# Linear attention with a smooth-ReLU MLP: an instruction order fixed by a list scheduler, transposes split between TensorE and DMA, and a new order of loads

## The chip, the cores and the metric

The kernel runs on one core of a Trainium2 chip. The metric is device time in microseconds (us), the median of several executions. The engines are named as the profile names them: PE (TensorE; PEld is its weight load), DVE (VectorE), ACT (ScalarE), POOL (GpSimd) and SP (SyncE, which here only issues DMA transfers; SPq is its queue).

## What is computed

The attention part is a linear recurrence over S = 768 steps for B = 4 batches, H = 8 heads and D = 48 channels; the MLP part takes the 3072 resulting rows of 384 numbers through 2048 hidden units and back.

```python
for t in range(S):                      # r, k, v: (4, 8, 768, 48); w, u: (8, 48)
    cur = np.einsum('bhd,bhe->bhde', u[None] * kt, vt)
    y[:, :, t] = np.einsum('bhd,bhde->bhe', rt, state + cur)
    state = w[None, :, :, None] * state + np.einsum('bhd,bhe->bhde', kt, vt)
x = y.transpose(0, 2, 1, 3).reshape(3072, 384)
h = x @ w_in                            # 384 -> 2048
g = np.where(h >= 1, h, np.where(h <= -1, 0.0, (h + 1) ** 2 / 4))
out = g @ w_out                         # 2048 -> 384, float32
```

## The kernel before

**Units.** The 768 steps are cut into 6 chunks of 128. A *unit* is one chunk of one batch, 128 rows by 8 heads; there are 24, chunk by chunk, the four batches inside a chunk. Two units make one MLP block of 256 rows, so there are 12 blocks. Unit i of batch b needs the state that unit i - 4 leaves.

**A unit's attention** is five calls:

- `prep` (L172 to L181): the unit's K, R and V (float32, 128 x 8 x 48, 192 KB each, loaded in pieces of 192 bytes) become K * Winv and R * Wpow (powers of w along the chunk, so that the decay becomes a product), in bfloat16 and padded from 48 to 64 columns a head; K * u * R, whose sum over a head is the diagonal term; and V in bfloat16. K * Winv and both products of K * u * R are on POOL; R * Wpow on DVE for units 0 to 5, later on POOL; V's cast on ACT for units 0 to 7, later on POOL.
- `s_tr` (L188, L190): eight 128 x 128 transposes on PE (two heads each) into PSUM, and a copy of all of them on ACT (L192) to a tile RK, which holds R and K transposed.
- `s_at` (L202): eight small matmuls, K against R, give the scores AT; DVE multiplies them with the causal mask (L206, two halves), and sums K * u * R over each head (L209). The next unit that is not yet loaded is loaded from here.
- `s_y`: y from the state (L220) and from AT and V (L223); the unit's own contribution to the state, st (L231); on DVE x = V * diagonal + y, head by head, eight instructions (L234); the state T is updated (L242, L244 on DVE, the decay L245 on POOL) and cast to Tbd (L248, ACT).
- `s_xp`: three transposes of x on PE (L255), a copy to xT (L257, ACT) and a sum of squares for a bound on |h| (L259, ACT).

**The MLP.** `layer1(m, n)` is one eighth of block m's hidden units: six matmuls (L270) and, on ACT, one Square (L276), which is the middle branch of the activation. `layer2(m, n)` is four matmuls (L288), two for each unit of the block; after the eighth piece the two outputs are copied (L292, one on DVE, one on ACT) and stored (L295). `w_norms` (L303 to L313) and `bound_fails` compute whether any |h| can pass 1; only then is the MLP done again with the full activation, which does not happen with this data.

**Weights.** w_in and w_out come as four quarters of 768 KB each (L106, L111) and are cast to bfloat16 by DVE and ACT (L337, L343).

**What sets the order.** The calls stand in the program in an order written by hand: one by one for blocks 0 to 2, then from a table `plan`, which puts the stages of unit i beside certain pieces of the MLP. All of it stands in one block, inside which the framework orders the instructions of each engine and the DMA issues by a model of its own of their times:

```python
    man.enter_context(tc.block(schedule_with_timeline_sim=True))
    ...
        g = max(m * nP - 15 + 4 * j, G0 - 5 + 3 * (i - 4 * UB))
        for s, at in enumerate((0, 2, 4, 7, 9)):
            plan.setdefault(max(g + at, G0), []).append((s, i))
```

Every DMA is issued from SP. K, R and V have six buffers each, the transposed and masked tiles three, the weights' float32 quarters four; of PSUM's eight banks the attention has four, layer 1 two and layer 2 two.

Of the kernel before, what the change touches and what calls it, by code (L numbers as in the profile page):

```python
# [11 lines left out]
ALU = mybir.AluOpType  # L12


@with_exitstack
def kernel(
# [11 lines left out]
    nc = tc.nc  # L28
# [13 lines left out]
    NB = B * NCH // UB  # L42
    LIM = 0.95
    mm = nc.tensor.matmul

    const = ctx.enter_context(tc.tile_pool(name="const", bufs=1))
    stage = ctx.enter_context(tc.tile_pool(name="stage", bufs=4))
    io = ctx.enter_context(tc.tile_pool(name="io", bufs=6))
    work = ctx.enter_context(tc.tile_pool(name="work", bufs=3))
    gpool = ctx.enter_context(tc.tile_pool(name="gpool", bufs=3))  # L50
    ewp = ctx.enter_context(tc.tile_pool(name="ewp", bufs=3))
    ps_h = ctx.enter_context(tc.tile_pool(name="ps_h", bufs=2, space=bass.MemoryType.PSUM))
    ps_o = ctx.enter_context(tc.tile_pool(name="ps_o", bufs=2, space=bass.MemoryType.PSUM))
    ps_a = ctx.enter_context(tc.tile_pool(name="ps_a", bufs=4, space=bass.MemoryType.PSUM))

    man = ExitStack()
    man.enter_context(tc.block(schedule_with_timeline_sim=True))


    units = [(b, c) for c in range(NCH) for b in range(B)]  # L60
    loaded = {}
    next_load = [0]

    def load():
        i = next_load[0]
        if i == len(units):
            return
        next_load[0] += 1
        b, c = units[i]
        t0 = c * C  # L70
        tiles = []
        for name, src in (("K", k), ("R", r), ("V", v)):
            t = io.tile([128, H, D], F32, name=name, tag=name)
            nc.sync.dma_start(out=t, in_=src[b, :, t0 : t0 + C, :].rearrange("h s d -> s h d"))
            tiles.append(t)
        loaded[i] = tiles
# [5 lines left out]
    nc.sync.dma_start(out=w_bc, in_=row_bcast(w))  # L82

    wc = const.tile([128, NP], F32, name="wc")
    nc.vector.memset(wc, 1.0)
    with nc.allow_non_contiguous_dma(reason="384 words"):
        for s in range(2):
            nc.sync.dma_start(
                out=wc[s * DP : s * DP + D, :],
                in_=w.rearrange("(p s) d -> s d p", s=2)[s],  # L90
            )
    load()
    u_bc = const.tile([128, H * D], F32, name="u_bc")
    nc.sync.dma_start(out=u_bc, in_=row_bcast(u))
    load()

# [6 lines left out]
    w_in_f, w_out_f = [], []  # L103
    for q in range(NQ):
        t = stage.tile([128, nKb, FQ], F32, name="w_in_f", tag="wf")
        nc.sync.dma_start(out=t, in_=w_in_src[:, :, q * FQ : (q + 1) * FQ])  # L106
        w_in_f.append(t)
        load()
    for q in range(NQ):
        t = stage.tile([128, TQ, d_out], F32, name="w_out_f", tag="wf")  # L110
        nc.sync.dma_start(out=t, in_=w_out_src[:, q * TQ : (q + 1) * TQ, :])  # L111
        w_out_f.append(t)


    ident = const.tile([128, 128], BF16, name="ident")
    make_identity(nc, ident)
    umask = const.tile([128, 128], F32, name="umask")
    nc.gpsimd.memset(umask, 0.0)
    nc.gpsimd.affine_select(
        out=umask, in_=umask, compare_op=ALU.is_ge, fill=1.0,  # L120
        base=0, pattern=[[-1, 128]], channel_multiplier=1,
    )
    ones = const.tile([128, 1], BF16, name="ones")
    nc.vector.memset(ones, 1.0)
    i_int = const.tile([128, 1], mybir.dt.int32, name="i_int")
    nc.gpsimd.iota(i_int, pattern=[[0, 1]], base=0, channel_multiplier=1)
    i_col = const.tile([128, 1], F32, name="i_col")
    nc.vector.tensor_copy(i_col, i_int)
    negj_col = const.tile([128, 1], F32, name="negj_col")
    nc.vector.tensor_scalar(negj_col, i_col, -1.0, -1.0, ALU.mult, ALU.add)  # L130
    lw = const.tile([128, H * D], F32, name="lw")
    nc.scalar.activation(lw, w_bc, AF.Ln)
    nc.scalar.activation(wc, wc, AF.Ln)
    Wpow = const.tile([128, H, D], F32, name="Wpow")
    nc.scalar.activation(Wpow.rearrange("p h d -> p (h d)"), lw, AF.Exp, scale=i_col)
    Winv = const.tile([128, H, D], F32, name="Winv")
    nc.scalar.activation(Winv.rearrange("p h d -> p (h d)"), lw, AF.Exp, scale=negj_col)  # L137
    nc.scalar.activation(wc, wc, AF.Exp, scale=float(C))
# [6 lines left out]
    NR = 4  # L145
    RWp, KWi = [], []
    for i in range(NR):
        for lst, nm in ((RWp, "RWp"), (KWi, "KWi")):
            t = const.tile([128, H, DP], BF16, name=f"{nm}{i}")
            nc.vector.memset(t, 0.0)  # L150
            lst.append(t)

    T = [const.tile([128, NP, D], F32, name=f"T{b}") for b in range(B)]
    Tbd = []
    for b in range(B):
        nc.gpsimd.memset(T[b], 0.0)
        t = const.tile([128, NP, 2 * D], BF16, name=f"Tbd{b}")
        nc.gpsimd.memset(t, 0.0)
        Tbd.append(t)
    xT = [const.tile([128, nKb, MT], BF16, name=f"xT{m}") for m in range(NB)]  # L160
    xn = const.tile([128, len(units)], F32, name="xn")
# [5 lines left out]
    ut = {}  # L167

    def prep(i):
        K, R, Vf = loaded.pop(i)  # L170
        Rw, Kw = RWp[i % NR], KWi[i % NR]
        nc.gpsimd.tensor_mul(Kw[:, :, 0:D], K, Winv)  # L172
        (nc.vector if i < 6 else nc.gpsimd).tensor_mul(Rw[:, :, 0:D], R, Wpow)
        KU = work.tile([128, H, D], F32, name="KU", tag="KU")
        nc.gpsimd.tensor_mul(KU, K, u3)  # L175
        nc.gpsimd.tensor_mul(KU, KU, R)  # L176
        V = work.tile([128, H, D], BF16, name="V", tag="V")
        if i < 8:
            nc.scalar.copy(V, Vf)
        else:  # L180
            nc.gpsimd.tensor_copy(V, Vf)  # L181
        ut[i] = [Rw, Kw, V, KU]

    def s_tr(i):
        Rw, Kw, V, KU = ut[i]
        tr = ps_a.tile([128, 2 * NP, 128], BF16, name="tr", tag="a")
        for p in range(NP):
            nc.tensor.transpose(tr[:, NP + p, :], pair(Kw, p), ident)  # L188
        for p in range(NP):
            nc.tensor.transpose(tr[:, p, :], pair(Rw, p), ident)  # L190
        RK = work.tile([128, 2 * NP, 128], BF16, name="RK", tag="RK")
        nc.scalar.copy(RK, tr)  # L192
        ut[i] = [Kw, V, RK, KU]

    def s_at(i):
        Kw, V, RK, KU = ut[i]
        RT, KT = RK[:, 0:NP, :], RK[:, NP : 2 * NP, :]
        AT_p = [ps_a.tile([128, NP, 128], F32, name=f"AT_p{s}", tag="a") for s in range(2)]
        for p in range(NP):
            for s in range(2):  # L200
                rows = slice(s * DP, s * DP + D)
# [143 lines left out]
    def each(m, ns, layer):  # L345
        for n in ns:
            layer(m, n)
# [142 lines left out]
```

## Time and profile before

| | |
|---|---|
| median of 3 runs | 200.91 us (200.70, 200.91, 202.21) |
| span of the profiled execution | 197.9 us (3.0 less than the median; its own time is this span and what lies around it, which the page does not show) |
| PE busy | 173.8 us, 88% of the span, 1818 matmuls |
| ACT, DVE, POOL busy | 136.0, 113.0 and 110.3 us |
| moved by DMA | 25.94 MB; most packets are under 512 bytes |

The page gives busy times, then the span in 40 slices, then the chain of work that ended last, then the costliest groups of instructions by line. The times are of one execution; the groups and the windows are means over many instructions. A line number is that of the kernel above.

### The profile page before, as it was taken

How to read it: one execution, taken by the hardware profiler on the slowest of the kernel's cores; microseconds unless marked ns; L12 is line 12 of the kernel's file. 1: busy time of each engine (PE TensorE's matmuls, PEld its weight loads, DVE VectorE, ACT ScalarE, POOL GpSimd, SP SyncE). 2: the span in 40 equal slices, each digit the busy share in tenths (PEclk: the TensorE clock that was granted, in tenths of full speed). 3: DMA queues.
4: the chain of work that ended last, by engine and by line, in shares of the span. 5: the costliest groups of instructions: out<-in, count | busy, mean ns of one | idle time of the engine just before them, and what ended most of it. 6: DMA issues, size and time to landing. Idle time of an engine off the chain costs nothing.

```text
span 197.9 us, 4831 instructions
## 1 busy us (share of the span) xinstructions
PE 173.8 (88%) x1818; PEld 129.5 (65%) x1818; DVE 113.0 (57%) x358; ACT 136.0 (69%) x275; POOL 110.3 (56%) x144
## 2 busy tenths in 40 slices
PE   0263697789999999999999999999999999999990
PEld 0141584677877677866687787686787777777750
DVE  4179999993777707952637647538457654331110
ACT  3657779899797826964787977866677776454540
POOL 7498664979797999994667846927513100000000
PEclk9999999999999999999999999999999999999999
DMA  4999999979999999999984400111011011020202
GB/s 97 200 253 262 252 232 182 257 134 246 223 213 267 176 187 174 254 187 237 228 182 81 120 3 23 59 39 45 2 43 40 3 40 43 0 80 0 84 3 89
DMA packets 82782, 25.94 MB, mean 131 GB/s; under 512 B 75841, under 2 KB 81217, under 8 KB 82753
## 3 DMA queue, kind: packets, MB, share of 16 engines
q1 hardware_dynamic: 82752, 25.57, 58.4%
q8 instruction: 16, 0.26, 0.6%
q14 instruction: 14, 0.11, 0.2%
HBM read 20.84 MB, written 4.72 MB: 129 GB/s over the span
## 4 chain that ended last, share of the span: by engine, by line
PE 67%; ACT 5%; DMA 3%; DVE 3%; issue 1%; ACTq 0%
PE o_p L288 30%; PE h_p L270 24%; DMA w_out_f<-in_moe_w_out_dram 3%; PE y L223 2%; ACT gT L276 2%; PE tr L190 2%; PE tr L188 2%; PE xp L255 1%; DVE x L234 1%; PE y L220 1%; PE st L231 1%; ACT RK L192 1%; PE n_p L309 1%; ACT w_out_sb L343 0%; DVE T_189 L242 0%
## 5 line engine op out<-in xcount | busy, mean ns | idle before, releaser
L276 ACT ACTIVATE gT<-h_p 128x512 bf16<-128x512 f32 x96 | 57.0, 598 | 38.1 <-PE h_p L270 37.3
L288 PE MATMUL o_p<-w_out_sb,gT 128*128 128x384 bf16 x384 | 73.5, 326 | 0.0
L270 PEld LDWEIGHTS <-w_in_sb 128*128 128x128 bf16 x576 | 53.8, 99 | 12.6 <-issue 1.0
L234 DVE SCALAR_TENSOR_TENSOR x<-V,diag,y 128x48 bf16<-128x48 bf16 x192 | 35.9, 258 | 23.7 <-PE y L223 18.9
L288 PEld LDWEIGHTS <-gT 128*128 128x128 bf16 x384 | 35.8, 98 | 18.4
L192 ACT COPY RK<-tr 128x1024 bf16<-128x1024 bf16 x24 | 24.4, 1015 | 3.7 <-PE tr L190 3.7
L175 POOL TENSOR_TENSOR KU<-K,u_bc 128x384 f32<-128x384 f32 x24 | 24.5, 1020 | 2.1 <-DVE diag L209 1.8
L176 POOL TENSOR_TENSOR KU<-KU,R 128x384 f32<-128x384 f32 x24 | 24.2, 1011 | 0.8
L292 DVE COPY o_sb<-o_p 128x384 f32<-128x384 f32 x12 | 6.7, 555 | 21.0 <-PE o_p L288 18.5
L209 DVE TENSOR_REDUCE diag<-KU 128x8 f32<-128x384 f32 x24 | 13.1, 548 | 5.8 <-POOL KU L176 5.3
L202 PEld LDWEIGHTS <-RK 48*128 48x128 bf16 x192 | 6.4, 98 | 10.1 <-ACT RK L192 4.7
L255 PE MATMUL xp<-ident,x 128*128 128x128 bf16 x72 | 10.7, 226 | 2.4 <-DVE x L234 2.3
L181 POOL CAST V<-V 128x384 bf16<-128x384 f32 x16 | 8.1, 504 | 7.2 <-PE h_p L270 4.7
L172 POOL TENSOR_TENSOR KWi_185<-K,Winv 128x384 bf16<-128x384 f32 x6 | 6.0, 998 | 8.2 <-PE st L231 5.2
L188 PE MATMUL tr<-ident,KWi_173 128*128 128x128 bf16 x24 | 2.9, 234 | 8.7 <-POOL KWi_173 L172 8.7
L172 POOL TENSOR_TENSOR KWi_173<-K,Winv 128x384 bf16<-128x384 f32 x6 | 6.0, 997 | 7.1 <-ACT Winv L137 3.5
L255 PEld LDWEIGHTS <-x 128*128 128x128 bf16 x72 | 6.4, 99 | 4.9 <-DVE x L234 3.6
L172 POOL TENSOR_TENSOR KWi_177<-K,Winv 128x384 bf16<-128x384 f32 x6 | 6.0, 997 | 4.6 <-DMA K<-in_k_dram 3.8
L172 POOL TENSOR_TENSOR KWi_181<-K,Winv 128x384 bf16<-128x384 f32 x6 | 6.8, 1132 | 2.7 <-DMA K<-in_k_dram 1.3
L270 PE MATMUL h_p<-xT_203,w_in_sb 128*128 128x256 bf16 x48 | 7.7, 309 | 0.4 <-DVE w_in_sb L337 0.3
L292 ACT COPY o_sb<-o_p 128x384 f32<-128x384 f32 x12 | 5.7, 477 | 2.8 <-PE o_p L288 2.7
L188 PEld LDWEIGHTS <-KWi_173 128*128 128x128 bf16 x24 | 1.9, 103 | 8.8 <-POOL KWi_173 L172 8.7
(366 smaller groups left out, 345.6 us busy)
## 6 DMA issues: line engine op xcount, KB each, us to landing
K<-in_k_dram SPq DMA_DIRECT2D x24, 192.0 KB, 4.9
R<-in_r_dram SPq DMA_DIRECT2D x24, 192.0 KB, 4.9
V<-in_v_dram SPq DMA_DIRECT2D x24, 192.0 KB, 4.5
out_dram<-o_sb SPq DMA_DIRECT2D x24, 192.0 KB, 2.9
w_in_f<-in_moe_w_in_dram SPq DMA_DIRECT2D x4, 768.0 KB, 6.1
w_out_f<-in_moe_w_out_dram SPq DMA_DIRECT2D x4, 768.0 KB, 6.1
w_bc<-in_w_dram SPq DMA_DIRECT2D x1, 192.0 KB, 3.5
u_bc<-in_u_dram SPq DMA_DIRECT2D x1, 192.0 KB, 4.4
```

Source lines behind the costliest of these rows:

```text
L172: nc.gpsimd.tensor_mul(Kw[:, :, 0:D], K, Winv)
L175: nc.gpsimd.tensor_mul(KU, K, u3)
L176: nc.gpsimd.tensor_mul(KU, KU, R)
L188: nc.tensor.transpose(tr[:, NP + p, :], pair(Kw, p), ident)
L192: nc.scalar.copy(RK, tr)
L209: nc.vector.reduce_sum(diag, KU, axis=mybir.AxisListType.X)
L234: nc.vector.scalar_tensor_tensor(x[:, h * D : (h + 1) * D], V[:, h, :], diag[:, h : h + 1], y[:, h, :], op0=ALU.mult, op1=ALU.add)
L255: nc.tensor.transpose(xp[:, kk, :], x[:, kk * 128 : (kk + 1) * 128], ident)
L270: mm(h_p[:, f, :], w_in_sb[:, kk, (2 * n + f) * 128 : (2 * n + f + 1) * 128], xT[m][:, kk, :], start=(kk == 0), stop=(kk == nKb - 1),)
L276: nc.scalar.activation(g, h_p, AF.Square, bias=0.5, scale=0.5)
L288: mm(o_ps[m][j], gT[m][:, f, j * C : (j + 1) * C], w_out_sb[:, f, :], start=(f == 0), stop=(f == nN - 1))
L292: (nc.scalar.copy if j else nc.vector.tensor_copy)(o_sb, o_ps[m][j])
```

## The change

**The order.** The kernel now holds a list scheduler. Each piece of work is an `Op` with the engines that may run it and an estimate of its time on each, what it depends on, the buffers that it takes and frees, and a due time. `Plan.run` goes through time: of all operations that could start within 0.02 us of the earliest, it places the one with the lowest due time, on the engine that would finish it first. The operations are then issued in order of their planned starts under `tc.manual_schedule()`, so that each engine's order and each buffer's slot are those of the plan. Casts of weights and of V, both products K * Winv and R * Wpow, the RK copies, the Tbd casts and the output copies may go to more than one engine.

```diff
-    man.enter_context(tc.block(schedule_with_timeline_sim=True))
+    man.enter_context(tc.manual_schedule())
+    slots = {
+        "a": 4, "h": 2, "o": 2,
+        "K": 6, "R": 6, "Vf": 6, "wf": 5, "KR": 4, "KU": 3, "V": 6, "RK": 4, "AT": 3, "P": 2, "VD": 3, "dg": 3,
+        "x": 5, "x2": 2, "g": 5, "os": 3, "sq": 2, "ss": 2,
+    }
+    def run(self):
...
+            t0 = min(c[0] for c in cand)
+            keyed = []
+            for est, ready, o, e, pl in cand:
+                key = o.due if not callable(o.due) else o.due(ready, last_mlp)
+                keyed.append(((key, est + o.engs[e][1]), est, o, e, pl))
+            best = None
+            for x in keyed:
+                if x[1] > t0 + 0.02 or best is not None and x[0] > best[0]:
+                    continue
+                best = x
...
+        done.sort(key=lambda o: o.start)
...
+    for o in P.run():
+        o.fn(o.eng)
```

**The loads.** Their order is a list; unit 0 and unit 1 stand first. The broadcasts of w and u and two small strided copies of them (wraw, uraw) are now issued from ACT.

```diff
+    ORDER = ["U0", "U1", "I0", "I1", "U2", "I2", "I3", "U3", "U4", "O0", "U5", "O1", "U6", "O2", "U7", "O3"]
+    ORDER += [f"U{i}" for i in range(8, NU)]
+    c_wbc = P.op("c_wbc", {"ACT": (0.6, 2.5)}, lambda e: nc.scalar.dma_start(out=w_bc, in_=row_bcast(w)), due=-100)
+    c_ubc = P.op("c_ubc", {"ACT": (0.6, 4.5)}, lambda e: nc.scalar.dma_start(out=u_bc, in_=row_bcast(u)), due=-94)
```

**The transposes.** K * Winv and R * Wpow of a unit now stand in one tile KR (128 x 16 x 64). Units 0 to 7 (`soft`, NS = 8) are transposed on PE as before; for units 8 to 23 a DMA on SP's queue transposes KR into RK (L418), and another transposes x into xT (L518).

```diff
+        soft = i < NS
+        both = {**pool(384), "DVE": (0.65, 0.7)}
...
+                nc.sync.dma_start_transpose(out=rkb.t, in_=krb.t.rearrange("p h d -> p (h d)"))
+            o_rk = P.op(f"trd{i}", {"SP": (1.7, 0)}, f_trd, deps=[o_kw, o_rw], uses=[krb], allocs=[rkb], due=D0 - 9, dma=1.4)
...
+                nc.sync.dma_start_transpose(out=xT[m][:, :, j * C : (j + 1) * C], in_=xb.t.rearrange("p h d -> p (h d)"))
```

**The diagonal.** For units 0 to 7 the product of the transposed R and K (L445, DVE) is multiplied with w * u by four small matmuls (L451) into spare columns of y's bank; K * u * R is not formed. For the others it is formed and summed as before. In both, V times the diagonal becomes a tile VD of its own (L457 on DVE, L475 on POOL), and x is one addition, y + VD (L500), in place of eight instructions.

```diff
-        for h in range(H):
-            nc.vector.scalar_tensor_tensor(
-                x[:, h * D : (h + 1) * D], V[:, h, :], diag[:, h : h + 1], y[:, h, :], op0=ALU.mult, op1=ALU.add
-            )
+                nc.vector.tensor_mul(pb.t, rkb.t[:, :NP, :], rkb.t[:, NP:, :])
...
+                    mm(yb.t[:, 384 + 2 * p : 386 + 2 * p], pb.t[:, p, :], uw[:, p, :], start=(p == 0), stop=False, skip_group_check=True)
...
+            nc.vector.tensor_add(xb.t, yb.t[:, 0:384].rearrange("p (h d) -> p h d", h=H), vdb.t)
```

**The MLP and the norms.** Layer 2 goes unit by unit, in four pieces of four matmuls (L597). The squares of w_in are added over the three row blocks on POOL (L632, L633), so that a norm needs two matmuls (L639) in place of six.

What that does to SP's queue around the last quarters of w_out (`w_out_f` before, `wf` in the new kernel, whose slots are named by number; `K`, `R` and `V` or `Vf` are a unit's loads). Before, behind eight units:

```order
L74 DMA K_460<-in_k_dram 128x8x48
L74 DMA R_462<-in_r_dram 128x8x48
L74 DMA V_464<-in_v_dram 128x8x48
L111 DMA w_out_f_139<-in_moe_w_out_dram 128x4x384
L74 DMA K_548<-in_k_dram 128x8x48
L74 DMA V_552<-in_v_dram 128x8x48
L74 DMA R_550<-in_r_dram 128x8x48
L111 DMA w_out_f_141<-in_moe_w_out_dram 128x4x384
L74 DMA K_659<-in_k_dram 128x8x48
L74 DMA V_663<-in_v_dram 128x8x48
L74 DMA R_661<-in_r_dram 128x8x48
L111 DMA w_out_f_143<-in_moe_w_out_dram 128x4x384
```

and now, behind six units, the second to the fourth quarter and units 6 and 7 between them:

```order
L363 DMA wf_0_521<-in_moe_w_out_dram 128x4x384
L326 DMA K_0_540<-in_k_dram 128x8x48
L326 DMA R_0_552<-in_r_dram 128x8x48
L326 DMA Vf_0_600<-in_v_dram 128x8x48
L363 DMA wf_1_630<-in_moe_w_out_dram 128x4x384
L326 DMA K_1_646<-in_k_dram 128x8x48
L326 DMA R_1_675<-in_r_dram 128x8x48
L326 DMA Vf_1_713<-in_v_dram 128x8x48
L363 DMA wf_2_750<-in_moe_w_out_dram 128x4x384
```

Eleven units stood ahead of the last quarter, now eight do.

SP's queue in the middle of the program, where it fetches the later units. Before, it holds loads and output stores:

```order
L74 DMA K_1384<-in_k_dram 128x8x48
L74 DMA V_1388<-in_v_dram 128x8x48
L74 DMA R_1386<-in_r_dram 128x8x48
L295 DMA out_0_dram<-o_sb_920 128x384
L295 DMA out_0_dram<-o_sb_917 128x384
L74 DMA K_1520<-in_k_dram 128x8x48
```

and now the transposes of KR and of x stand between them:

```order
L518 DMA_TRANSPOSE xT5_99<-x_0_1282 128x3x128
L611 DMA out_0_dram<-os_0_952 128x384
L418 DMA_TRANSPOSE RK_0_1342<-KR0_82 128x8x128
L611 DMA out_0_dram<-os_1_1042 128x384
L518 DMA_TRANSPOSE xT5_99<-x_1_1369 128x3x128
L418 DMA_TRANSPOSE RK_1_1408<-KR1_83 128x8x128
L326 DMA K_2_1434<-in_k_dram 128x8x48
```

A load now stands behind transposes that wait for DVE's and POOL's products.

DVE in the same phase (T2 is the state of batch 2; `KR3`, `a_0` and the like are slots). Before, a unit has eight small additions for x, its share of the state, the sum, two masks and an output copy:

```order
L234 SCALAR_TENSOR_TENSOR x_1476<-V_1214,diag_1382,y_1458 128x48 x8
L242 TENSOR_TENSOR T2_189<-T2_189,st_1471 48x192 x2
L209 TENSOR_REDUCE diag_1783<-KU_1655 128x8
L206 TENSOR_TENSOR AT0_1514<-AT_p0_1504,umask_150 128x512
L206 TENSOR_TENSOR AT1_1516<-AT_p1_1505,umask_150 128x512
L292 COPY o_sb_1443<-o_p_1195 128x384
```

and now:

```order
L390 TENSOR_TENSOR KR3_85<-K_5_1004,Winv_80 128x8x48
L543 TENSOR_TENSOR T2_88<-T2_88,a_3_1082 48x192 x2
L500 TENSOR_TENSOR x_3_1131<-a_0_1109,VD_2_1052 128x384
L394 TENSOR_TENSOR KR3_85<-R_5_1050,Wpow_79 128x8x48
L435 TENSOR_TENSOR AT1_0_1138<-a_2_1136,umask_73 128x512
L435 TENSOR_TENSOR AT0_0_1137<-a_1_1135,umask_73 128x512
L470 TENSOR_REDUCE dg_2_1182<-KU_2_1104 128x8
```

The eight additions have become one, and products of K and R that stood on POOL (L172, L173) are among DVE's work.

More of the change, by code (lines that the diff above doesn't have):

```diff
@@ L141 @@
     umask4 = umask[:, None, :].to_broadcast([128, NP, 128])
[L145 to L159, printed above, removed]
@@ L160, with copy @@
[L160 to L161 removed]
+    halves = [slice(s * DP, s * DP + D) for s in range(2)]
+    V_ENG = {"ACT": nc.scalar, "DVE": nc.vector, "POOL": nc.gpsimd}
+    def copy(eng, o, i):
+        (nc.scalar.copy if eng == "ACT" else V_ENG[eng].tensor_copy)(o, i)
     def pair(t, p):
         return t[:, 2 * p : 2 * p + 2, :].rearrange("q h d -> q (h d)")
[L167 to L179, printed above, removed]
[L180 to L182 removed]
```

779 lines of the change are left out of this document (476 added, 303 removed).

## The prediction

> **What bounds the kernel now.** I read the page first: the busy times and the slices of TensorE (PE) and of the DMA engines.
>
> ```profile
> PE 173.8 (88%) x1818; PEld 129.5 (65%) x1818; DVE 113.0 (57%) x358; ACT 136.0 (69%) x275; POOL 110.3 (56%) x144
> ...
> PE   0263697789999999999999999999999999999990
> ...
> DMA  4999999979999999999984400111011011020202
> ```
>
> A slice is 4.95 us. PE has gaps in the first ten or so and none after; the DMA engines are full in those same slices and run empty half way. So there are two stages: a front that waits for data, and a long stage in which PE never stops. The view of busy time by stretches puts numbers on it (length, then PE, weight loads, DVE, ACT, POOL, clock, DMA share, GB/s):
>
> ```profile
> 0.00:10.00 10.00, 1.03 (x8) 0.77 (x8) 2.85 (x13) 5.22 (x9) 5.76 (x21) 1.00 0.79 149
> 10.00:20.00 10.00, 5.47 (x53) 3.27 (x54) 8.96 (x27) 6.53 (x13) 8.71 (x9) 1.00 1.07 257
> ...
> 60.00:80.00 20.00, 19.73 (x205) 14.61 (x203) 11.63 (x37) 12.31 (x26) 18.43 (x23) 1.00 1.05 194
> ```
>
> The chain that ended last says where the second stage begins and ends (start, length, what); the timeline adds PE's last group and the two stores behind it.
>
> ```profile
> 62.87 1.41 PE o_p L288 x8
> ...
> 190.60 1.96 PE o_p L288 x12
> ...
> 190.44 2.11 PE L288 MATMUL o_p<-w_out_sb,gT 128*128 128x384 bf16 x12
> 192.85 1.34 SPq L295 DMA_DIRECT2D out_dram<-o_sb  x2
> ```
>
> From 62.87 on the chain is PE alone. PE ends at 192.6, the span at 197.9: a tail of 5.3. The span is 3.0 below the median of the runs, 200.91; I add that 3.0 to every span below.
>
> **What a piece of PE work costs.** While PE never stops, the distance from one start to the next is the price. Two stretches of the timeline, unit 18 or so, hold every kind:
>
> ```profile
> 142.22 0.23 PE L202 MATMUL AT_p_2630<-RK 48*128 48x128 bf16 x1
> ...
> 142.55 1.64 PE L288 MATMUL o_p<-w_out_sb,gT 128*128 128x384 bf16 x9
> 144.02 0.82 PE L270 MATMUL h_p<-xT_211,w_in_sb 128*128 128x256 bf16 x6
> 144.67 1.14 PE L288 MATMUL o_p<-w_out_sb,gT 128*128 128x384 bf16 x6
> 145.65 0.33 PE L255 MATMUL xp<-ident,x 128*128 128x128 bf16 x3
> 145.82 0.82 PE L270 MATMUL h_p<-xT_211,w_in_sb 128*128 128x256 bf16 x6
> 146.47 0.39 PE L188 MATMUL tr<-ident,KWi_173 128*128 128x128 bf16 x4
> ...
> 146.92 0.82 PE L270 MATMUL h_p<-xT_211,w_in_sb 128*128 128x256 bf16 x6
> 147.57 0.33 PE L220 MATMUL y<-Tbd_201,RK 128*128 128x96 bf16 x4
> ...
> 147.95 0.33 PE L231 MATMUL st<-V,KWi_185 128*128 128x96 bf16 x4
> 148.12 0.82 PE L270 MATMUL h_p<-xT_211,w_in_sb 128*128 128x256 bf16 x6
> ...
> 128.43 0.23 PE n_p L309 x6
> ```
>
> So: the eight AT matmuls 0.33, nine o_p 1.47 (0.163 each), a layer-1 piece 0.65, the three xp 0.17, the eight tr 0.45, y 0.38 (0.21 without the state), st 0.17, a norm 0.23. All of before: 24 x (0.45 + 0.33 + 0.17) + 20 x 0.38 + 4 x 0.21 + 20 x 0.17 + 96 x 0.65 + 384 x 0.163 + 8 x 0.23 = 161.6 us. PE ends at 192.6, so 31 us of its time went idle, nearly all in the front.
>
> **Part one, the transposes.** Sixteen units lose tr and xp: 16 x 0.62 = 9.9 us. The norms keep two of six matmuls: 8 x 0.15 = 1.2 less. Added are eight groups of four diagonal matmuls (128 columns of weights, 2 of data), which the trace does not show: between four of the y matmuls (0.11) and the four st (0.17), I take 0.15, 1.2 in all. New total 151.7, or 9.9 less. With the old idle time that alone would give 191.
>
> **Part two, the front.** What PE waits for there is the last quarter of w_out. Issues on the queue, and when the first w_in and the last w_out quarter were picked up:
>
> ```profile
> 8.65 0.74 SPq L106 DMA_DIRECT2D w_in_f<-in_moe_w_in_dram  x1
> ...
> 25.39 0.80 SPq L106 DMA_DIRECT2D w_in_f<-in_moe_w_in_dram  x1
> ...
> 56.47 0.76 SPq L111 DMA_DIRECT2D w_out_f<-in_moe_w_out_dram  x1
> ...
> 65.70 0.72 SPq L74 DMA_DIRECT2D K<-in_k_dram  x1
> ...
> 74.80 0.94 SPq L74 DMA_DIRECT2D K<-in_k_dram  x1
> ...
> 14.59 0.62 ACT L337 CAST w_in_sb<-w_in_f 128x512 bf16<-128x512 f32 x1 [0.62 <-DMA w_in_f<-in_moe_w_in_dram]
> ...
> 61.95 0.56 DVE L343 CAST w_out_sb<-w_out_f 128x768 bf16<-128x768 f32 x1 [0.92 <-DMA w_out_f<-in_moe_w_out_dram]
> ```
>
> From 8.65 to 25.39 the queue took three quarters and three units: 5.58 a pair. From 65.70 to 74.80 it took three units: 3.03 each. A weight quarter is the rest, 2.55 (786 KB, 308 GB/s); a unit's 590 KB go at 195. Before, nine units and seven quarters lie between the two pick-ups: 9 x 3.03 + 7 x 2.55 = 45.1, measured 47.4. Now six units do: 36.0. The bytes ahead of the first quarter stay (w, u, two units), a little sooner started: 14.3. So the last quarter lands at **50.3**, and with two casts each on ACT and POOL its first user runs at **51.5** instead of 62.9.
>
> That gain is smaller than it looks, since before filled its wait with other work. In the new order PE has ahead of that user 18 layer-1 pieces, 12 o_p matmuls, eight tr, eight AT, eight st, seven dg, seven y and seven xp: 25.5 us. Behind it lie 126.2. In the stretch from 60 to 80 PE was busy 19.73 of 20, so I add 1.7 for small gaps: PE would end at **179.4** if nothing else set the pace.
>
> **Part three, the middle.** The order puts attention far ahead: behind unit 23's AT stand 25 layer-1 pieces, 152 o_p matmuls, y and norms, 41.9 us. So 126.2 - 41.9 = 84.3 us of PE work hold the attention of 16 units, and what feeds them must keep up: 5.3 us a unit.
>
> *DMA.* A unit's loads cost 3.03, its share of ten stores 0.40 (192 KB at the rate of the quarters, 0.64 each), and its two transposes (256 and 96 KB) are not in the trace. By the rate of the quarters they cost 1.17, by that of the units' loads 1.85; if the transposed pieces were half as long as a load's, at the same time a piece, 3.7. I take 1.85, the row whose pieces are short. 16 x 5.28 = 84.5 from 50.3, and 2.5 for landing (w_bc below, 3.5, less 1.0 of transfer): unit 23's AT at 137.3, PE's end 179.2, the same as PE's own path.
>
> ```profile
> w_bc<-in_w_dram SPq DMA_DIRECT2D x1, 192.0 KB, 3.5
> ```
>
> *POOL and DVE.* POOL starts its products 0.96 apart; 60 of them from unit 8 on, with the small work about 76, are under 84. On DVE one addition replaces eight small ones per unit (258 ns each), but 20 products of two SBUF operands come to it in this stage:
>
> ```profile
> 67.94 1.00 POOL L172 TENSOR_TENSOR KWi_173<-K,Winv 128x384 bf16<-128x384 f32 x1
> 68.90 1.00 POOL L175 TENSOR_TENSOR KU<-K,u_bc 128x384 f32<-128x384 f32 x1
> ...
> L234 DVE SCALAR_TENSOR_TENSOR x<-V,diag,y x192: 254/258/266, 14.2 to 176.0; 128x48 bf16<-128x48 bf16 x192
> ...
> L173 DVE TENSOR_TENSOR RWp_171<-R,Wpow x2: 559/914/1269, 7.1 to 29.2; 128x384 bf16<-128x384 f32 x2
> L173 DVE TENSOR_TENSOR RWp_175<-R,Wpow x2: 865/1092/1319, 11.4 to 35.5; 128x384 bf16<-128x384 f32 x2
> ...
> L173 DVE TENSOR_TENSOR RWp_179<-R,Wpow x1: 546/546/546, 18.0 to 18.0; 128x384 bf16<-128x384 f32 x1
> L173 DVE TENSOR_TENSOR RWp_183<-R,Wpow x1: 1351/1351/1351, 23.0 to 23.0; 128x384 bf16<-128x384 f32 x1
> ```
>
> The six take 0.55 when POOL rests and up to 1.35 beside it, 0.99 in the mean: 0.44 more than alone, 8.7 us for 20. The Trainium skill, SBUF — State Buffer, "SBUF: two separate sides", has DVE and GpSimd share one port pair as an exclusive lock, which a DVE operation with two SBUF inputs and a GpSimd operation hold in turn. The rows agree, and by that rule each of the 20 can wait out a POOL product, which speaks against this part of the change; the sum takes the excess from the rows. DVE has room for it, but a late product makes a late transpose, and PE runs in a fixed order. I let a quarter reach the path: 2.2.
>
> **The sum.** 179.4 + 2.2 = 181.6 for PE's end, tail 5.3, 3.0 around the span: **190 us**. The casts, RK copies and diagonal work moved among ACT, DVE and POOL I cost at nothing: ACT loses 22 of 24 RK copies, and layer-2 pieces cover PE while one is late; uncovered, the second rival prices it.
>
> **Rivals.**
> *The queue is quicker* (0.22). The shortest unit interval, 65.70 to 68.37, was 2.67, the shortest pair 5.09; then 6 x 2.67 + 7 x 2.42 = 33.0, the last quarter at 47.3, first user 48.5, no slip: **185**. For it: SP no longer waits for buffers. Against: the DMA share stood at 1.07.
>
> ```profile
> 68.37 1.30 SPq L74 DMA_DIRECT2D K<-in_k_dram  x1
> ...
> 14.32 0.78 SPq L106 DMA_DIRECT2D w_in_f<-in_moe_w_in_dram  x1
> 19.41 0.76 SPq L106 DMA_DIRECT2D w_in_f<-in_moe_w_in_dram  x1
> ```
>
> *DVE's excess reaches PE whole* (0.19), as waits of y for the mask and of AT for the transpose: 8.7 in place of 2.2, **196**; with POOL's half of it (products of 1.3 in place of 1.0), 203.
>
> *The transposes set the pace, and it is slower* (0.10). PE's wait is at AT (L429) for RK (L418). With t for a unit's transposes the time is 160.1 + 16 t: 190 at 1.85, slower than before by 1% from 2.7, **219** at 3.7. Against: nothing in the rows makes a transposing transfer dearer than a strided load; for: no row shows one. The Trainium skill, DMA: Bandwidth & Descriptors, "Latency and other measured facts", gives transposing DMAs 261 GB/s; an estimate by that page is 1.38 a unit, and the sum would then be PE's own path. VectorE: DVE Perf Modes in the Trainium skill, "The three transpose paths", gives 1309 ns for a 128x128 block by DMA against 390 on TensorE; eleven blocks one after another would be 14.4 a unit, an estimate by that page, and would put the time near 390. Its TensorE figure is seven times this trace's 56 ns a block in a stream, so I read both as latencies of one alone.
>
> *That the order isn't what it says* is out: the printed order has the transposes gone and the loads moved.
>
> **How the numbers follow.** Forecast 187 to 193 with 0.45; 180 to 187 0.22; under 180 0.04; 193 to 203 0.19; above 0.10. A measurement of this kernel tells about 1% (2 us) from no change. Faster holds all below 198.9, two thirds of the 193 to 203 case among it: 0.84; within 1% 0.06; slower 0.10. The range leaves out a little of the quick side and the slow transposes: 181 to 203.
>
> **What would show it.** The first o_p that needs the last w_out quarter near 51.5; PE's busy time near 160 against 173.8; PE's end near 181.6; unit 23's AT near 138, with 42 us of unbroken layer work behind it. Waits of AT for RK, growing unit by unit, would mean slow transposes; waits of y for AT's mask, DVE. The prediction is wrong if the transposes take over 2.7 a unit, if loads wait on SP behind a transpose that isn't ready, or if the front is short of something other than weights.

## The result, and the profile after

The changed kernel takes **195.2 us** (193.1 to 196.3) against 201.0 of the kernel before: a ratio of 0.968 with a 95% interval of 0.961 to 0.974, 5.8 us less. The forecast was 190, the range 181 to 203. The profiled execution below was the longest of the four timed ones, 196.34 us for a span of 194.4, so 1.1 above the median, and a difference of about 1 us between an instant in it and the same instant in another run says little.

The page of the changed kernel: busy times, PE and DMA in 40 slices (now of 4.86 us), and its DMA queue.

```profile
span 194.4 us, 4322 instructions
PE 164.1 (84%) x1642; PEld 121.0 (62%) x1642; DVE 110.5 (57%) x223; ACT 107.9 (55%) x226; POOL 106.8 (55%) x155
...
PE   0453984988999997998997989799979999999990
...
DMA  5999999989899968898797988888776211111121
...
q1 hardware_dynamic: 105600, 30.94, 70.5%
```

PE's busy time fell from 173.8 to 164.1, by 9.7, where the prediction priced 9.9. But the unbroken row of nines that before has from its tenth slice on is gone: there are eights and sevens until the thirtieth. The DMA engines, which ran empty half way before, now work until there. The stretches say the same (length, PE, weight loads, DVE, ACT, POOL, clock, DMA share, GB/s):

```profile
60.00:80.00 20.00, 18.68 (x209) 13.76 (x208) 15.44 (x31) 11.76 (x29) 16.42 (x19) 1.00 0.93 174
80.00:100.00 20.00, 19.31 (x215) 14.24 (x213) 11.70 (x23) 13.15 (x29) 16.46 (x24) 1.00 0.86 169
100.00:120.00 20.00, 17.66 (x178) 12.98 (x176) 13.43 (x28) 12.71 (x28) 16.08 (x21) 1.00 0.84 174
120.00:140.00 20.00, 18.28 (x193) 13.40 (x192) 14.66 (x28) 11.54 (x25) 17.07 (x23) 1.00 0.89 190
```

Three instants split the span: PE's first use of the last w_out quarter, unit 8's and unit 23's AT (from PE's timeline), and its last group (from the chain that ended last).

```profile
52.10 0.81 PE L597 MATMUL o<-w_out_sb,g 128*128 128x384 bf16 x4
...
60.34 0.40 PE L429 MATMUL a<-RK 48*128 48x128 bf16 x8
...
147.19 0.40 PE L429 MATMUL a<-RK 48*128 48x128 bf16 x8
...
180.37 9.11 PE o L597 x56
```

PE's work by the prediction's prices is 151.7 us, and it ends at 189.5, so 37.8 us of it are idle: 26.6 until 52.1 (25.5 of work are done by then), 11.2 behind that. Before, 31.0 were idle, nearly all until 62.9. So PE ends 3.1 us earlier: 9.9 less work and 4.4 less idle time in the front, against 11.2 of new gaps. The tail (4.9 in place of 5.3) and what lies around the span (1.9 in place of 3.0) are 1.5 shorter; that makes 4.6 for this execution, and the median is 1.1 below it. The 3.0 is not a property of the kernel before: in its executions beside the experiments, time less span is 1.7 to 2.6. By them, its profiled execution was itself some 0.4 to 1.3 quicker than the median, and part of the 1.1 is a difference between executions.

What PE waited for from 52 to 150 (total, times, longest):

```profile
PE h L574 <- ACT g L586: 1.9, 2, 1.2
PE a L536 <- DVE V L242: 1.6, 2, 1.3
PE o L597 <- DVE os L242: 1.3, 1, 1.3
PE a L536 <- ACT V L242: 1.2, 2, 0.9
PE a L536 <- POOL V L242: 0.8, 1, 0.8
PE a L485 <- DVE VD L457: 0.5, 1, 0.5
PE a L429 <- DMA RK<-KR: 0.4, 1, 0.4
```

These are 7.7 us, and they are all of PE's gaps behind 52.1. The other 3.5 of the 11.2 are work that took longer than its price. Nearly half of the 7.7 is st (L536) waiting for the cast of a V. ACT's own waits from 52 to 150 show where that came from: it stood 3.9 us for V to land, and from 60 to 140 the casts of V on DVE stood 4.6.

```profile
ACT V L242 <- DMA Vf<-in_v_dram: 3.9, 5, 1.2
```

So the question for the experiments was why V lands late in the middle: because loads stand on SP behind transposes that wait for their products, because the transposes fill the DMA path, or because POOL and DVE are slow to free buffers. The other suspect was the clock: the timed executions of this kernel are shorter the higher their mean granted clock (193.1 at 0.991, 195.2 at 0.982, 196.3 at 0.978).

### The profile page after: what moved, and what is told of

The parts are those of the page before. It is cut to its first block, busy times and chain, and to the rows that moved or that the text cites. A ratio compares the mean times of both kernels' runs of the same rounds, so it can differ in the third digit from the quotient of the medians.

```text
span 194.4 us, 4322 instructions
## 1 busy us (share of the span) xinstructions
PE 164.1 (84%) x1642; PEld 121.0 (62%) x1642; DVE 110.5 (57%) x223; ACT 107.9 (55%) x226; POOL 106.8 (55%) x155
## 3 DMA queue, kind: packets, MB, share of 16 engines
q1 hardware_dynamic: 105600, 30.94, 70.5%
## 4 chain that ended last, share of the span: by engine, by line
PE 45%; DMA 20%; DVE 12%; POOL 8%; SPq 6%; ACT 4%; issue 3%; DVEq 0%; POOLq 0%; ACTq 0%
PE h L574 19%; PE o L597 19%; DMA Vf<-in_v_dram 7%; DMA R<-in_r_dram 6%; DVE AT L435 4%; DMA K<-in_k_dram 4%; SPq L326 4%; DMA out_dram<-os 3%; PE a L409 2%; POOL VD L475 2%; POOL KR L394 2%; POOL KU L465 2%; DVE x L500 2%; POOL KU L464 1%; PE a L488 1%
## 5 line engine op out<-in xcount | busy, mean ns | idle before, releaser
L574 PE MATMUL h<-xT,w_in_sb 128*128 128x256 bf16 x576 | 79.6, 277 | 2.4 <-ACT g L586 1.9
L597 PE MATMUL o<-w_out_sb,g 128*128 128x384 bf16 x384 | 75.7, 326 | 1.3 <-DVE os L242 1.3
L586 ACT ACTIVATE g<-h 128x512 bf16<-128x512 f32 x96 | 56.0, 593 | 32.0 <-PE h L574 30.7
L597 PEld LDWEIGHTS <-g 128*128 128x128 bf16 x384 | 35.7, 98 | 17.7 <-issue 1.4
L435 DVE TENSOR_TENSOR AT<-a,umask 128x512 bf16<-128x512 f32 x48 | 30.8, 682 | 6.5 <-PE a L429 6.3
L526 ACT ACTIVATE x<-x 128x384 bf16<-128x384 bf16 x24 | 12.5, 522 | 16.8 <-DVE x L500 16.7
L394 POOL TENSOR_TENSOR KR<-R,Wpow 128x384 bf16<-128x384 f32 x16 | 16.6, 1039 | 6.7 <-DMA R<-in_r_dram 5.5
L500 DVE TENSOR_TENSOR x<-a,VD 128x384 bf16<-128x384 f32 x24 | 13.3, 552 | 8.9 <-PE a L488 8.4
L475 POOL TENSOR_TENSOR VD<-V,dg 128x384 f32<-128x384 bf16 x16 | 13.6, 855 | 6.6 <-DVE dg L470 3.2
L390 DVE TENSOR_TENSOR KR<-K,Winv 128x384 bf16<-128x384 f32 x16 | 11.3, 709 | 9.1 <-DMA K<-in_k_dram 6.0
L536 PE MATMUL a<-V,KR 128*128 128x96 bf16 x80 | 7.3, 219 | 5.0 <-ACT V L242 2.6
L536 PEld LDWEIGHTS <-KR 128*128 128x128 bf16 x80 | 5.6, 105 | 6.6 <-issue 6.2
```

The source lines that it names most:

```text
L394: V_ENG[e].tensor_mul(krb.t[:, :H, 0:D], Rb.t, Wpow)
L435: nc.vector.tensor_mul(atb.t[s], at_p[s].t, umask4)
L475: nc.gpsimd.tensor_mul(vdb.t, vb.t, dgb.t[:, :, None].to_broadcast([128, H, D]))
L500: nc.vector.tensor_add(xb.t, yb.t[:, 0:384].rearrange("p (h d) -> p h d", h=H), vdb.t)
L536: mm(stb.t[:, p, :], pair(krb.t[:, H:, :], p), pair(vb.t, p), start=True, stop=True)
L574: mm(hb.t[:, f, :], w_in_sb[:, kk, (2 * n + f) * 128 : (2 * n + f + 1) * 128], xT[m][:, kk, :], start=(kk == 0), stop=(kk == nKb - 1),)
```

## The experiments

Twelve variants gave times; each is compared with the kernel before. The changed kernel's 0.968 is the mark.

**The clock.** Ahead of certain PE operations of the first 45 us extra matmuls on a zero tile go into an unused bank.

```diff
+    WARM = {"tr0": 10, "at0": 1, "dg0": 1, "tr1": 1, "st1": 4, "dg1": 3, "xp0": 1, "xp1": 4, "L1_0_0": 2, "y2": 3,
+            "at3": 2, "dg3": 2, "tr4": 2, "y3": 2, "xp3": 1, "y5": 3}
     for o in P.run():
+        for _ in range(WARM.get(o.name, 0)):
+            mm(dp, dz[:, 0:128], dz, start=True, stop=True)
         o.fn(o.eng)
```

> Orders as in the changed kernel, but PE runs 42 extra matmuls on a zero tile into a bank that is not yet used, where it stood idle ahead of certain operations of the first 45 us, so that it is busier there. The changed kernel's granted clock falls to 0.50 from 32.4 to 39.2; its timed runs have a mean clock of 0.978 to 0.991 and are shorter the higher it is (196.3, 195.2, 193.1). Theory clock (the half-clock stretch follows PE's idle time and its loss reaches the end): no such stretch, clock 0.99 or more, time 191 to 192. Theory front-by-data (PE waits for data there anyway, and the stretch is a by-product): 194 to 196 even if the clock stays full; or the stretch appears elsewhere.

195.9 us (ratio 0.974, 0.966 to 0.982). The stretch from 30 to 40 of the changed kernel, and of this one:

```profile
30.00:40.00 10.00, 8.10 (x89) 6.05 (x84) 7.82 (x17) 6.03 (x12) 4.62 (x8) 0.66 0.95 247
```

```profile
30.00:40.00 10.00, 8.43 (x106) 5.50 (x105) 9.20 (x20) 6.26 (x14) 4.70 (x7) 1.00 0.92 234
```

The half-clock stretch is gone, and the time is no shorter; unit 23's AT came at 146.5. So PE waits for data there either way, and although shorter executions had a higher clock, the clock was not what made them shorter, as far as this run shows.

**The front undone.** Units 8 to 10 go ahead of the last three w_out quarters again.

```diff
-"U4", "O0", "U5", "O1", "U6", "O2", "U7", "O3"]
+"U4", "O0", "U5", "U6", "U7", "U8", "O1", "U9", "O2", "U10", "O3"]
```

> The list of loads as before in its middle: units 8, 9 and 10 go ahead of the last three w_out quarters, so that eleven units stand ahead of the last one in place of eight; the plan is made anew with that. By the prediction's second part the last quarter lands three units later, 3 x 3.03 = 9.1 us, its first user near 61, and as PE then has up to 7 us of other work to put ahead, the time is 197 to 204. Theory that the middle is paced by the loads of the later units (SP or DMA), not by the weights: these units now come 9 us earlier, which is worth the same in the middle, and the time is 194 to 197.

199.2 us (197.2 to 200.3; ratio 0.994, 0.991 to 0.998), 4 us slower than the changed kernel. The fourth quarter's first user:

```profile
62.28 0.81 PE L597 MATMUL o<-w_out_sb,g 128*128 128x384 bf16 x4 [2.33 <-DVE w_out_sb L242]
```

It moved by 10.2, three units at 3.4. Less than half of that reached the end: in the profiled execution, the quickest of the ten, unit 23's AT came at 145.4, 1.8 earlier than in the changed kernel, with 3 us more of PE's time behind it. The order of loads is worth some 4 us.

**The transposes made tiny.** Same plan and orders, same number of DMAs in SP's queue, but plain copies of 256 bytes. Matmuls then read what older units left, so RK's four buffers become fixed tiles, and xT has four tiles used in turn in place of twelve.

```diff
-                nc.sync.dma_start_transpose(out=rkb.t, in_=krb.t.rearrange("p h d -> p (h d)"))
+                nc.sync.dma_start(out=rkb.t[0:1, 0, :], in_=krb.t[0:1, 0:2, :].rearrange("p h d -> p (h d)"))
-                nc.sync.dma_start_transpose(out=xT[m][:, :, j * C : (j + 1) * C], in_=xb.t.rearrange("p h d -> p (h d)"))
+                nc.sync.dma_start(out=xT[m][0:1, 0, j * C : (j + 1) * C], in_=xb.t.rearrange("p h d -> p (h d)")[0:1, 0:128])
```

> Plan and orders as in the changed kernel, transposes still issued from SP behind the same products, but each moves 256 bytes and transposes nothing: the later units work on transposed tiles that are left from the first eight, so the result leaves out their transposes. Theory DMA (traffic of the transposes, 5.8 MB, 24 us of queue time, sets the pace of the middle): AT of unit 23 near 138, time 187 to 189. Theory SP (it is the waiting for the products in SP's queue that holds the loads): the waits stay, only the issue price of 1.2 us becomes some 0.6, time 192 to 195. Theory products: 194 to 196.

The whole took 560.0 us (ratio 2.789), since the stale tiles put the bound on |h| over 1 and the MLP ran a second time behind all else; only the stretch ahead of that is read. Its windows and unit 23's AT:

```profile
60.00:80.00 20.00, 20.00 (x226) 14.73 (x224) 16.82 (x32) 13.17 (x31) 18.67 (x23) 1.00 0.53 112
80.00:100.00 20.00, 19.86 (x218) 15.09 (x217) 15.14 (x28) 13.34 (x31) 18.19 (x24) 1.00 0.61 135
100.00:120.00 20.00, 19.45 (x204) 14.13 (x204) 15.61 (x31) 13.69 (x29) 17.83 (x27) 1.00 0.64 140
120.00:140.00 20.00, 20.00 (x211) 14.80 (x208) 13.82 (x26) 13.38 (x29) 18.93 (x22) 1.00 0.49 119
```

```profile
139.78 0.40 PE L431 MATMUL a<-RKc 48*128 48x128 bf16 x8
```

PE is full, and unit 23's AT is 7.4 us earlier. From unit 8's AT (60.5) the pace is 5.29 us a unit, the 5.3 that the prediction gave PE's work alone; in the changed kernel it is 86.9 / 15 = 5.79. So nearly all of the middle's gaps come from the transposes, and POOL and DVE, with the same products as in the changed kernel, keep up: that theory falls. Whether it is the transposes' traffic or SP's time for issuing them the run does not tell, since an issue fell from 1.24 and 1.18 us at least to 0.50.

**The transposes on ACT's queue.** Plan and orders unchanged, `nc.sync` becomes `nc.scalar` in L418 and L518.

```diff
-                nc.sync.dma_start_transpose(...)
+                nc.scalar.dma_start_transpose(...)
```

> The plan, every other engine's order and all buffers as in the changed kernel; only the 32 transposing DMAs are issued from ACT's queue in place of SP's. The changed kernel takes 195.2 (193.1 to 196.3), unit 23's AT starts at 147.2, and PE has 11 us of gaps behind its first use of the last w_out quarter. Theory SP (loads come late because they stand on SP behind transposes that wait for their products): loads come earlier, AT of unit 23 near 138 to 141, time 187 to 190, unless ACT itself now waits at the transposes, which would show as waits of PE for g. Theory DMA (the transposes' traffic fills the DMA engines): nothing changes, 194 to 196. Theory products (POOL and DVE are the pace): nothing changes, 194 to 196.

197.6 us (ratio 0.984, 0.976 to 0.991), unit 23's AT at 148.1. SP issued the last V 13 us earlier (122.4 for 135.9), but ACT now stood at its own issues, and PE waited 3.4 us for g from 52 to 150 in place of 1.9. ACT's waits at its own issues, over the whole span:

```profile
ACT V L242 <- issue: 5.2, 6, 1.5
ACT g L586 <- issue: 4.2, 7, 0.8
```

One wait was traded for another, so the time doesn't separate SP from the DMA engines. The windows say more. From 60 to 100, in the changed kernel and then in this one:

```profile
60.00:100.00 40.00, 37.98 (x422) 28.00 (x421) 27.14 (x54) 24.91 (x57) 32.88 (x43) 1.00 0.89 171
```

```profile
60.00:100.00 40.00, 35.28 (x372) 25.49 (x370) 28.63 (x51) 23.28 (x54) 32.92 (x42) 1.00 1.29 225
```

Fed from two queues, with the loads running ahead, the DMA engines moved 225 GB/s in place of 171. So in the changed kernel they had room in this stretch.

**The loads ahead in SP's queue.** Two runs keep the plan and the order of all compute engines, and emit the loads of units 10 to 23 earlier on SP, by up to 6 and up to 10 us of planned time (the second with eight buffers for K, R and V and four activation tiles in place of five).

```diff
+    HOIST = lambda i: min(6.0, 1.0 * (i - 9))        # the second: min(10.0, 1.5 * (i - 9))
...
+            o.moved = max([o.start - HOIST(i), o3.start + 0.001, ...] + [u.start + 0.001 for u in (old.users if old else [])])
...
+    for o in sorted(seq, key=lambda o: getattr(o, "moved", o.start)):
+        o.fn(o.eng)
```

> The plan is the changed kernel's, and PE, ACT, DVE and POOL have its order; only on SP the loads of units 10 to 23 stand earlier among the transposes and stores, by up to 6 us of planned time (one to two places of a unit; three units in place of two are loaded ahead of most transposes). Traffic and issue prices stay. In the changed kernel the DMA engines stood at 0.84 to 0.93 from 60 to 140 while PE waited 3.7 us in all for casts of a V that came late, and unit 23's AT came at 147.2. Theory SP's order (a load waits in SP's queue behind a transpose whose products aren't there, and the DMA engines stand idle meanwhile): DMA share over 0.95 in the middle, AT of unit 23 near 142 to 144, time 190 to 193. Theory throughput (the transposes' own time on the DMA engines or their issue sets the pace): 147, 194 to 196. Theory products or ACT: 194 to 196.

> As the run before, but by up to 10 us of planned time, and with eight buffers each for K, R and V (the activation tiles four in place of five). Theory SP's order: AT of unit 23 near 139 to 142, 188 to 191, if the transposes don't now come late behind the loads (waits of AT for RK); throughput: 194 to 196; slower than 196 if late transposes outweigh it, as where six units were loaded ahead.

198.3 us (0.991, 0.987 to 0.995) and 197.3 (0.983, 0.975 to 0.991): slower, not faster, with unit 23's AT at 149.7 and 149.5. PE's waits from 52 to 150 in the first of them:

```profile
PE a L429 <- DMA RK<-KR: 5.2, 4, 2.8
PE o L597 <- POOL w_out_sb L242: 0.9, 1, 0.9
PE a L536 <- ACT V L242: 0.7, 1, 0.7
```

The waits for V became waits for RK. In the first run PE's clock also fell to 0.91 from 80 to 100; in the second it stayed at 1.00 from 60 to 140, and it was no better. Whatever goes first, the other is late: the theory of SP's order falls. What is left is something that loads and transposes share, SP's time for issuing or the DMA engines.

**Loads replanned further ahead.** The plan made anew with earlier due times, eight buffers and four activation tiles.

```diff
-D_m[i // UB] - 16 + 2 * (i % UB)
+D_m[i // UB] - 36 + 2 * (i % UB)
-        "K": 6, "R": 6, "Vf": 6
+        "K": 8, "R": 8, "Vf": 8
```

> Loads of units 8 to 23 get due times 20 us earlier and K, R and V eight buffers each in place of six (the activation tiles four in place of five), so that six units in place of two are loaded ahead of unit 8's transpose; the traffic and the number of DMAs stay. With the transposes' traffic taken out, unit 23's AT came at 139.8 in place of 147.2 and PE had no gaps from 60 to 140; with the transposes on another queue, at 148.1. Theory late V (the gaps are waits for a V that was loaded too late, so that the DMA engines, at 0.84 to 0.93 in the middle, have room to load ahead): AT of unit 23 near 141, time 188 to 191. Theory throughput (loads, transposes and stores need the DMA engines or SP's issue time about as long as PE needs for its work): the first gaps move later, but unit 23's AT stays at 145 to 148, time 194 to 196.

200.3 us (0.996, 0.992 to 1.001). Unit 23's AT did come at 139.5, but unit 8's at 70.6 in place of 60.3, behind the loads of four more units, and the new plan left 51 us of PE's work behind unit 23's AT in place of 42. The early part paid for the late one.

**x back on PE.** Only RK is transposed by DMA.

```diff
-        if soft:
+        if True:
             xpb = Buf("a")
```

> x of every unit is transposed on PE, as the first eight are; only RK of units 8 to 23 is transposed by DMA. That takes 16 DMAs of 96 KB and 1.2 us of SP's time each away, and adds 16 x 0.17 = 2.7 us to PE and 16 copies of 0.5 to ACT or DVE. Theory throughput (DMA engines or SP at the same pace as PE): the gaps in the middle shrink by more than is added, AT of unit 23 near 144, time 191 to 194. Theory RK alone (the gaps come from RK's transposes, not from x's): time 196 to 199.

196.4 us (0.979, 0.973 to 0.984). PE's waits from 52 to 150 fell from 7.7 to 3.6, and unit 23's AT came at 135.1 with more PE work behind it; the 2.7 us of added PE work and copies took the rest. Even.

**All on PE, and the transposes alone.** First NS = 24 in the changed kernel; then the kernel before with only the transposes of units 8 to 23 moved to DMA.

```diff
-    NS = 8
+    NS = 24
```

> All 24 units are transposed on PE and have their diagonal by matmul; no transposing DMA is left; the scheduler and the order of loads stay. PE gets 16 x (0.62 + 0.15) = 12.3 us more, K * u * R goes from POOL. By the prediction's prices PE ends at 52 + 126.2 + 12.3 + some 1 to 2 = 192, time 197 to 199: within 1% of the kernel before, so that the transposes by DMA are worth all of what the middle gives, and the new loads the rest. If the DMA transposes cost as much as they save (7.4 us of gaps against 9.9 us of PE work), this is 196 to 198 all the same; under 194 would mean that the transposes are a loss.

```diff
+        if i >= 8:
+            RK = work.tile([128, 2 * NP, 128], BF16, name="RK", tag="RK")
+            nc.sync.dma_start_transpose(out=RK, in_=KRt[i % NR].rearrange("p h d -> p (h d)"))
...
+        if i >= 8:
+            nc.sync.dma_start_transpose(out=xT[m][:, :, j * C : (j + 1) * C], in_=x)
```

> The kernel before with one part of the change: units 8 to 23 have RK and x transposed by DMA from SP (K * Winv and R * Wpow stand in one tile for that); order by the framework, loads, diagonal, x in eight instructions and norms as before. PE loses 16 x 0.62 = 9.9 us. Before, PE was saturated from 62.9 on. If the transposes are hidden as well as in the changed kernel (7 of 9.9 given back), 198 to 199; if the loads, which here run seven units ahead, hide them whole, 190 to 192; if SP's order by the framework holds transposes up, slower than 201.

All on PE: 207.5 us (1.040, 1.031 to 1.048), some 9 us above my 198. The transposes alone: 204.1 (1.017, 1.010 to 1.024). Neither part is a gain by itself: the new order without the transposes by DMA is 7.0 us slower than before, the transposes without the new order 3.5 slower, and both together 5.8 faster. In the second, PE lost most from 80 to 100, with the clock at 0.83 there:

```profile
80.00:100.00 20.00, 16.49 (x143) 10.19 (x143) 14.47 (x45) 6.28 (x19) 16.83 (x21) 0.83 1.06 204
```

In the first, DVE was busy 39.0 of the 40 us from 60 to 100, so it is the likely limit there; no run tests that. I have not taken either loss apart further.

**The fixed order.** The same plan as the program's order, but inside the framework's own scheduling block.

```diff
-    man.enter_context(tc.manual_schedule())
+    man.enter_context(tc.block(schedule_with_timeline_sim=True))
```

> All operations, engines and buffers of the changed kernel in the order of its plan, but inside the framework's own scheduling block, which orders each engine and SP by its own model, as in the kernel before. If the fixed order is what makes the transposes by DMA pay (in the framework's order, on the kernel before, they cost 3.4 us: 204.05 against 200.6): 199 to 204. If the order is worth little, 194 to 197.

213.4 us (1.070, 1.060 to 1.079), worse than either expectation: with these operations, the fixed order is worth 18 us against the framework's.

**Larger pieces.** Orders, transposes, bytes and number of DMAs as in the changed kernel, but the later units are read in pieces of 1536 bytes.

```diff
+                    flat_src = src[b].rearrange("h s d -> (h s d)")[t0 * H * D : (t0 + C) * H * D]
+                    nc.sync.dma_start(out=t, in_=flat_src.rearrange("(p h d) -> p h d", p=C, h=H))
```

> Plan and order of every engine and of SP, buffers, number of DMAs and bytes as in the changed kernel; but K, R and V of units 8 to 23 are read as one contiguous stretch, in pieces of 1536 bytes in place of 192, so the later units work on rows in the wrong order and the result leaves out their right placing. At the rate of the weights' quarters a unit's loads take 1.9 us of the DMA engines in place of 3.0; the transposes keep their traffic, their issue on SP and their landing. So far: with the transposes' traffic and 0.7 of their 1.2 us issue taken away AT of unit 23 came at 139.8 in place of 147.2; with the loads moved ahead in SP's queue at 149.7, waits for V having become waits for RK. Theory throughput (loads and transposes share DMA engines that have little more time than PE needs): 1.1 us a unit taken from the loads is as good as taken from the transposes, AT of unit 23 near 140, time 187 to 190. Theory issue (the 1.2 us that SP takes for each transpose) or latency (their landing): AT stays at 145 to 148, time 193 to 196.

**190.35 us** (0.951, 0.945 to 0.958). Windows, unit 23's AT, and what is left of PE's waits from 52 to 150:

```profile
60.00:80.00 20.00, 20.00 (x224) 14.75 (x224) 16.52 (x31) 12.94 (x32) 18.35 (x22) 1.00 0.71 171
80.00:100.00 20.00, 20.00 (x225) 15.17 (x220) 14.97 (x27) 13.26 (x29) 18.27 (x25) 1.00 0.80 200
100.00:120.00 20.00, 19.28 (x205) 14.10 (x202) 15.50 (x32) 13.69 (x30) 17.83 (x26) 1.00 0.81 204
120.00:140.00 20.00, 19.94 (x201) 14.55 (x199) 14.24 (x26) 13.55 (x30) 19.03 (x23) 1.00 0.83 192
```

```profile
140.24 0.40 PE L433 MATMUL a<-RK 48*128 48x128 bf16 x8
```

```profile
PE o L601 <- POOL w_out_sb L242: 1.1, 1, 1.1
PE h L578 <- ACT g L590: 0.7, 1, 0.7
```

With the transposes untouched, cheaper loads give the same 7 us back. So what the middle runs out of lies on the path that loads and transposes share. That path has two parts, SP's issuing and the DMA engines' moving, and no run changes one without the other: longer pieces also shorten SP's issue of a load (from 60 to 140, medians of 0.57, 0.63 and 0.63 for K, R and V become 0.43, 0.44 and 0.43, together 0.5 us a unit, as much as the middle had lost).

The kept traces point to SP. From 60 to 140 the records of its issues add up to 74.4 of the 80 us in the changed kernel, and to 63.8 here, 52.5 with the tiny copies and 39.2 in the kernel before; such a record can hold a wait besides the issue. The DMA engines did not slow down: in the changed kernel a load lands 3.5 or 3.6 us after its issue (medians of that stretch),

```profile
K<-in_k_dram SPq DMA_DIRECT2D x12, 192.0 KB, 3.6
RK<-KR SPq DMA_TRANSPOSE x13, 3.3
```

while it is 3.4 to 3.8 here and with the tiny copies, 4.0 to 4.5 in the kernel before, and 4.6 to 5.2 with the transposes on ACT's queue, where the engines did more. An experiment that shortens the issues and leaves the traffic was not run, so this stays a reading. The variant with larger pieces is no kernel to use, since it reads the wrong rows; none that computes the reference beat the changed one.

## Why the prediction was right, and where it was off

- **PE's prices and the 9.9 us: right.** With the transposes out of the way the pace is 5.29 a unit for the 5.3 forecast, and from unit 23's AT to PE's end there are 42.3 us for 41.9.
- **The front: right.** First use of the last quarter at 52.1 for 51.5; idle until then 26.6 for 26.0. Undoing it cost 4.
- **The middle: the step that failed.** It is "unit 23's AT at 137.3, PE's end 179.2, the same as PE's own path". AT of unit 23 came at 147.2, and behind 52.1 PE lost 11.2 us where I had 3.9 (1.7 small gaps and 2.2 for DVE). That is 7.3 us, of which a tail and a rim 1.5 shorter than assumed gave some back. The 84.5 us of DMA time were about right: the queue's busy share went from 58.4% of 197.9 (115.6 us) to 70.5% of 194.4, and with the 2.7 of the broadcasts that moved to ACT's queue that is 24.2 more, 1.51 for a unit's transposes where I took 1.85. But the sum left out two things. I took the larger of two chains of 84 us as their joint time, and I priced a transfer by its bytes alone, with no term for SP, which issues all of them one after another. By the medians from 60 to 140 a unit's three loads, two transposes and its share of the stores cost SP 4.8 us of the 5.3 that PE needs, before any wait for a product. Making the transposes' DMAs tiny, or the loads' pieces longer, took the loss away; which of the two it was, SP or the engines, stays open, with the traces on SP's side.
- **DVE's products: the 2.2 on the path were not there.** The durations were as read (541, 616 and 1222 ns, least, median and most, for K * Winv on DVE). One reading was too simple: of the two quick products of before, only the one at 7.11 had POOL at rest; the one at 17.98 ran into POOL's at 18.13, which then took 1.25. But with the same products and tiny transposes PE hardly waits: 0.8 us from 52 to 150.
- **The rivals.** The quicker queue did not show, and neither did DVE's excess. Transposes that are slow by their own price fell: 1.51 a unit, near the 1.38 that I had estimated by the Trainium skill, DMA: Bandwidth & Descriptors, "Latency and other measured facts". What did happen lies near a case that I had only as a sentence of what would make the prediction wrong, loads that wait on SP behind a transpose.
- **The range: in part luck.** The time fell in the stretch from 193 to 203, which had 0.19 and was meant for DVE's excess (196). That excess did not happen, so it is the width of the range, and not the rival, that holds 195.2. Of the 11 us forecast, 5.8 came.

The rim of 3.0 around the span set the median of before against one execution whose own time is not known; in the timed executions of before beside the experiments it is 1.7 to 2.6, and in those of the changed kernel 1.8 to 1.9.

## What to carry to other kernels

When two paths' needs for a stage come out about equal, don't take the larger as the stage's time. Here both were priced at 5.3 us a unit and the stage took 5.8; relieving the DMA path gave the difference back. Price a transfer twice, by what the DMA engines need to move it and by what the issuing queue needs to start it. Moving work from the full engine to a queue that looks half empty over the whole span pays only as far as that queue has room in the same stage. And parts of such a change can each lose by themselves and gain together, so test them apart before crediting one.

## What the runs showed of the hardware

A transposing DMA costs SP 1.24 us at least for 128 x 1024 and 1.18 for 128 x 384, where a load costs 0.57 to 0.63 (medians from 60 to 140) and the 256-byte copy 0.50; it lands 3.3 and 2.4 us after its issue (medians).

```profile
L418 SPq DMA_TRANSPOSE RK<-KR x16: 1237/1256/3073, 55.4 to 143.6; - x16
...
L518 SPq DMA_TRANSPOSE xT<-x x16: 1183/1208/3052, 65.9 to 150.8; - x16
```

The granted clock's column does not show that matmuls ran slowly at the start. The same eight transposes took 1.13 us at 10.54 and 0.61 at 49.20, both with a clock of 1.00 in the windows:

```profile
10.54 1.13 PE L409 MATMUL a<-ident,KR 128*128 128x128 bf16 x8 [0.48 <-DVE T L545]
...
49.20 0.61 PE L409 MATMUL a<-ident,KR 128*128 128x128 bf16 x8
```

The Trainium skill, TensorE: Matmul & The Clock Gate, "What's actually happening", has the gate at half rate by default and after an idle window of 3.4 us. The trace agrees with the first: until about 21 matmuls take 1.5 to 1.9 times as long as later (eight for AT 0.61 in place of 0.40, six of layer 1 1.44 in place of 0.82). The second it neither shows nor contradicts: the stretch at half rate from 32.4 to 39.2 comes behind gaps, but PE was busy 2.26 of the 4 us from 28 to 32. With filler matmuls in the gaps the clock stayed at 1.00 from 30 to 40.
